# Row sums copied into the output page by ScalarE, and a new order of the first four slots, in a block attention with a gated MLP on one Trainium2 core

## Chip, cores and metric

The kernel runs on one core of one Trainium2 chip. The metric is the device time of one execution in microseconds (us). Three runs of the kernel before gave 791.10, 791.16 and 791.66 us; their median is 791.16 us. The profiled execution, from which all rows below come, took 792.08 us.

## What is computed

```
scores = q @ k.T / 8                     # 8 batches x 8 heads, 576 positions, head size 64
scores = where(block_i >= block_j, scores, -1e9)     # blocks of 64 positions
attn   = exp(scores - max) / (sum(exp) + 1e-9)
x      = attn @ v                        # heads side by side: 576 x 512 per batch

h      = gelu_tanh(x @ w_in)             # 512 -> 1024, halves u and v
v_n    = (v - mean) / sqrt(var + 1e-6) * g_ln
v_s    = w_sg @ v_n + b_sg               # over positions, 576 x 576
out    = x + (u * v_s) @ w_out
```

Inputs and outputs are 32-bit floats (two of the weights arrive as 64-bit and are narrowed in the kernel). Products need nearly full 32-bit precision, so most operands are split into a high and a low half of a rounded type, and a product is three matmuls: high by high, high by low, low by high.

## The kernel before, in words

**Slots.** Two heads of one batch make a pair; there are 32 pairs, and `slot(n, sc)` (line 743) works on pair n. A slot does two things at once: it finishes the attention of pair n (`Values`), and it makes the scores of pair n+1 (`Scores`). A batch is four slots. After the fourth slot of a batch, `begin` puts the batch's feed-forward part into a queue of generators, `work`, and each later call of `hole()` (line 722) in a slot issues one step of it, about a dozen or more matmuls. The first four slots have no such work: `hole()` does nothing there.

**Scores.** The 576 query rows lie in five tiles, 0 to 4. `step1` (S1) makes the first 288 columns of tile 4 and all of tile 1, `step2` (S2) the rest of tile 4, `step3` (S3) tiles 3 and 0, `step4` (S4) tile 2, each for both heads. The three terms of a product are issued in the order high-high, high-low (`k_l`), low-high (`q_l`). The result stands in a PSUM bank of tag `s` (five banks). VectorE takes the row maximum and writes the scores to SBUF (`maximum`, line 338); ScalarE makes the exponents and their sums (`exponents`). `split_qk` (line 127) makes the halves of the next pair's q and k: VectorE casts `qk_h`, then GpSimd subtracts to get `qk_l`, first for k and then for q. There is one buffer of each.

**Values.** TensorE transposes the exponents block by block into PSUM banks of tag `p` (three banks): `turn0` (bank `pa`, one for each head), `turn2` with `turn2_rest` (`pb`, two), `turn1` with `turn1_rest` (`pc`, two), `turn_first` (`pd`). ScalarE or VectorE copies each bank to SBUF (`pt`), and `av0`, `av2`, `av1`, `av00` multiply with v and accumulate in the bank `ob` (of tag `s`) and, for the first 64 rows, in columns 256 to 320 of `pd`, the tile `t4`. The inverse row sums are made by `inverse` at the start of a slot (VectorE `ri`, GpSimd `rx`), and `turn_sums` (line 461) transposes them into columns 128 to 256 of `t4` and into a bank `pe`, the tile `rp`. `normalise` (line 492) then has ScalarE copy `ob` and `o0` into a page `x` in SBUF, has VectorE multiply it with the sums in `pe` and `t4`, and stores the page to DRAM (`spill`). `split` (line 502) makes its halves `xh` (VectorE, with a small piece for the last rows by GpSimd) and `xl` (GpSimd) for the feed-forward part. Pages `x` share three buffers with `xr`, the pages that are loaded back for the residual.

**Order.** TensorE's instructions are kept in the order of the program (`PIN = "P"`, line 58). For the other engines a planner orders the instructions when the kernel is built, by readiness in its own simulation and, among ready ones, by program order. The engines then run these lists strictly in order. An instruction that waits holds up all that stand behind it on its engine. Dependencies inside PSUM are kept by bank: a write to one part of a bank waits for a read of another part of it.

**Weights.** They are loaded and narrowed in pieces, and `weight_step` issues one: for `w_in` that is a DMA, two instructions on ScalarE, three on VectorE and one on GpSimd. They stand behind the newest maximum and exponent that had been issued at that point. `load_share(n, k)` is called in a slot at four places, k = 0 to 3, and divides the slot's count `WS[n]` (2, 2, 2, 1 in the first four slots, 10 in slot 4) among them. With a count of two that is one piece at k = 1, in the slot's middle behind S1 and S2, and one at k = 3, behind `normalise`; the one of slot 3 comes at k = 3.

Of the kernel before, what the change touches and what calls it, by code (L numbers as in the profile page):

```python
# [9 lines left out]
F32 = mybir.dt.float32  # L10
# [4 lines left out]
ALU = mybir.AluOpType  # L15
# [13 lines left out]
def kernel(  # L29
# [13 lines left out]
    B, H, D, S = qT.shape  # L43
    P = 128
    BLK = 64
# [23 lines left out]
    def page(dtype, n, name):  # L69
        tag, bufs = KINDS.get(name, KINDS["w"])  # L70
        return sp.tile([P, n], dtype, tag=tag, name=name, bufs=bufs)

    def bank(tag, name, bufs):
        return psum.tile([P, 512], F32, tag=tag, name=name, bufs=bufs)

    def sbank(name):
        return bank("s", name, 5)

    def pbank(name):
        return bank("p", name, 3)  # L80
# [3 lines left out]
    def pin(ins, e):  # L84
        return tc.keep_in_program_order(ins) if e in kept else ins
# [4 lines left out]
    def turn(out, in_, identity):  # L90
        return pin(nc.tensor.transpose(out, in_, identity), "P")  # L91
# [11 lines left out]
    V, A, G, SP = Pinned(nc.vector, "V"), Pinned(nc.scalar, "A"), Pinned(nc.gpsimd, "G"), Pinned(nc.sync, "S")  # L103

    def copy(e, dst, src):
        return {"v": V.tensor_copy, "a": A.copy, "g": G.tensor_copy}[e](dst, src)
# [8 lines left out]
    def load_qk(n):  # L115
        b, h = PAIRS[n]
        if n == 0:

            q_f, k_f = page(F32, S, "w"), page(F32, S, "w")
        else:  # L120
            t = sp.tile([P, 2, S], F32, tag="qk_f", name="qk_f", bufs=1)
            q_f, k_f = t[:, 0, :], t[:, 1, :]
        SP.dma_start(q_f, qT[b, h : h + 2].rearrange("a d s -> (a d) s"))
        SP.dma_start(k_f, kT[b, h : h + 2].rearrange("a d s -> (a d) s"))
        qk[n] = (q_f, k_f) if n == 0 else t

    def split_qk(n):
        t = qk[n]
        hi = sp.tile([P, 2, S], F32R, tag="qk_h", name="qk_h", bufs=1)
        lo = sp.tile([P, 2, S], F32R, tag="qk_l", name="qk_l", bufs=1)  # L130
        V.tensor_copy(hi, t)
        for i in (1, 0):
            G.tensor_tensor(lo[:, i, :], t[:, i, :], hi[:, i, :].bitcast(F32), op=ALU.subtract)
        q_h, k_h, q_l, k_l = hi[:, 0, :], hi[:, 1, :], lo[:, 0, :], lo[:, 1, :]
        qk[n] = [(q_h, k_h), (q_h, k_l), (q_l, k_h)]

    def load_v(n):
        b, h = PAIRS[n]
        v_f = v_bufs[n % 2]
        cols = slice(h * D, (h + 2) * D)  # L140
        SP.dma_start(
            v_f[:, : NT - 1, :],
            v[b, : (NT - 1) * P, cols].rearrange("(j p) d -> p j d", p=P),
        )
        SP.dma_start(v_f[:TAIL, NT - 1, :], v[b, S - TAIL :, cols])
        vals[n] = v_f
# [6 lines left out]
    t = sbank("warm")  # L153
# [15 lines left out]
    for s in (0, 1):  # L169
        t = cp.tile([P, NT, 2 * D], F32, name=f"v_f{s}")  # L170
# [5 lines left out]
    for s in range(4):  # L176
        row = []
        for i in range(NT):
            t = cp.tile([P, P * (i + 1) if i else BLK], F32, name=f"prob{s}_{i}")
# [106 lines left out]
    def weight_step():  # L286

        with ExitStack() as stack:
            for ins in newest.values():
                stack.enter_context(tc.issue_after(ins.ins))  # L290
            while weights and next(weights[0][1], None) is None:
                weights.popleft()
# [96 lines left out]
    class Values:  # L389
# [71 lines left out]
        def turn_sums(self):  # L461

            turn(self.t4[:, 128:256], self.rx[:, 0, :], ident)
            t = self.rp = pbank("pe")
            for i in range(1, NT):
                turn(t[:, (i - 1) * P : i * P], self.rx[:, i, :], ident)

        def av(self, dst, j, pts, c0, n, start, stop):
            for a in (0, 1):
                r = slice(a * D, (a + 1) * D)  # L470
                mm(dst[r, :], self.v[:, j, r], pts[a][:, c0 : c0 + n], start=start, stop=stop)
# [19 lines left out]

        def normalise(self):

            x = self.x = page(F32, S, "x")
            copy("a", x[:, BLK:], self.ob)
            copy("a", x[:, :BLK], self.o0)
            V.tensor_tensor(x[:, BLK:], self.rp, x[:, BLK:], op=ALU.mult)
            V.tensor_tensor(x[:, :BLK], self.t4[:, 128:192], x[:, :BLK], op=ALU.mult)
            spill[self.b, self.p] = dp.tile([P, S], F32, tag="spill", name="spill", bufs=12)
            SP.dma_start(spill[self.b, self.p], x)  # L500

# [14 lines left out]
    def run_side(k):  # L516

        while k > 0 and side and side[0][0] != "G":
            k -= 1
            side.popleft()[1]()  # L520

    def run_gelu():

        if side and side[0][0] == "G":
            side.popleft()[1]()
# [196 lines left out]
    def hole(k=1):  # L722

        while k > 0 and work:
            try:
                next(work[0])
                k -= 1
            except StopIteration:
                work.popleft()

    WS = [2, 2, 2, 1, 10, 3, 3, 3, 2]

    def load_share(n, k):

        if n < len(WS):
            for _ in range(WS[n] * (k + 1) // 4 - WS[n] * k // 4):
                weight_step()

    PLAN = ["1111111", "1111111", "1111111", "1111112"]
# [3 lines left out]
    def slot(n, sc):  # L743
        va = Values(n, sc)
        nx = Scores(n + 1) if n + 1 < N else None
        g = [int(x) for x in (FIRST if n // 4 == 1 else PLAN)[n % 4]]
        if n + 2 < N:
            load_qk(n + 2)
        if n + 1 < N:
            load_v(n + 1)  # L750
        va.inverse()
        va.turn0(0)
        va.turn0(1)
        hole(g[0])
        load_share(n, 0)
        run_side(2)

        va.turn2()
        va.turn2_rest()
        if nx:  # L760
            nx.step1()
            nx.step2()
        va.av0()
        if nx:
            nx.exponents(1, 4)
        va.turn1()
        hole(g[1])
        load_share(n, 1)
        run_side(2)
        hole(g[2])  # L770
        run_side(2)
        va.turn1_rest()
        va.turn_first()
        if nx:
            nx.step3()
            nx.step4()
        va.av2()
        va.turn_sums()
        if nx:
            nx.exponents(3, 0, 2)  # L780
        hole(g[3])
        load_share(n, 2)
        run_side(2)
        va.av1()
        va.av00()
        hole(g[4])
        va.normalise()

        wait = n // (H // 2) > 0 and n % (H // 2) < 2
        pending.append(va.split)  # L790
        if not wait:
            while pending:
                pending.popleft()()
        run_side(2)
        if n + 2 < N:
            split_qk(n + 2)
        load_share(n, 3)
        hole(g[5])
        run_gelu()
        run_side(3)  # L800
        hole(g[6])
        run_side(3)
        if n % (H // 2) == 1:
            while pending:
                pending.popleft()()
        return nx
# [19 lines left out]
    for n in range(N):  # L826
        sc = slot(n, sc)
        if n % (H // 2) == H // 2 - 1:

            def begin(b=PAIRS[n][0]):  # L830
                v_, u_, s_, o_ = feed_forward(b)

                work.extend([v_, u_, *last_o, s_])
                last_o[:] = [o_]

            begin()
# [45 lines left out]
```

## Time and profile before

| | |
|---|---|
| median of three runs | 791.16 us |
| profiled execution | 792.08 us, of which the span from first to last instruction is 790.2 us |
| mean granted TensorE clock | 0.978 |
| slot 0 (first transpose to first transpose) | 9.83 to 25.51 us |
| slot 1, slot 2, slot 3 | 25.51 to 41.68, to 55.93, to 70.25 us |
| slot 4, the first with feed-forward steps | 70.25 to 106.45 us |
| VectorE and ScalarE busy, whole span | 63% and 57% |

A slot's limits are read from a timeline. Each row has a start in us, a duration, engine, line and operation, then what is written from what, the shapes and a count; a note in brackets gives the idle time of the engine ahead of it and what ended that. Almost all instructions carry line 88, 91 or 101, those of the helpers that record them, so rows are told apart by their tiles. The row of a stretch (`A:B`) gives its length, the busy time of each engine with its count of instructions, then the granted TensorE clock (1.00 is full), the share of the DMA engines and GB/s.

### The profile page before, as it was taken

What the parts mean: (1) busy time and instruction counts of PE and PEld (TensorE: products, weight loads), DVE (VectorE), ACT (ScalarE), POOL (GpSimd) and SP (SyncE); (2) the same over time, 40 slices, a digit from 0 to 9 for tenths busy, and PEclk for the clock granted to TensorE, in tenths of its full rate; (3) what the DMA queues carried; (4) which work ended last, traced back from release to release, by engine and by line L of the source; (5) the groups of instructions that cost most, each with busy time, mean ns of one, the idle gap of its engine ahead of it and who ended that gap; (6) DMA issues with size and microseconds to landing.
All of it is one profiled execution on the core that took longest, in us unless ns stands there. A gap on an engine that the chain in (4) does not pass through costs nothing. (4 is left out here: it accounts for less than half of the span.)

```text
span 790.2 us, 15821 instructions
## 1 busy us (share of the span) xinstructions
PE 761.1 (96%) x5926; PEld 639.9 (81%) x5926; DVE 499.7 (63%) x1457; ACT 450.0 (57%) x1172; POOL 267.9 (34%) x331
## 2 busy tenths in 40 slices
PE   7777998999999999999999999999999999999998
PEld 5554786877888888887888888888888978888998
DVE  5897578885757466563866648565676647633532
ACT  4775689567844478435974368544793358721600
POOL 4354255552424113351133414231233510322121
PEclk9897799999999999999999999999999999999999
DMA  7143224212241024311042122410233101320042
GB/s 239 61 126 118 89 91 141 88 61 75 78 149 60 2 76 122 106 61 52 25 136 90 61 76 62 145 50 32 77 106 121 61 19 59 105 76 31 1 121 75
DMA packets 46911, 65.66 MB, mean 83 GB/s; under 512 B 4082, under 2 KB 22514, under 8 KB 46836
## 3 DMA queue, kind: packets, MB, share of 16 engines
q1 hardware_dynamic: 46836, 64.67, 25.6%
q8 instruction: 46, 0.75, 0.4%
q14 instruction: 29, 0.24, 0.1%
HBM read 45.78 MB, written 18.87 MB: 82 GB/s over the span
## 5 line engine op out<-in xcount | busy, mean ns | idle before, releaser
L101 ACT ACTIVATE prob<-prob,negm 128x448 f32<-128x448 f32 (+4 forms) x320 | 176.4, 554 | 40.6 <-DVE negm L101 37.1
L101 POOL TENSOR_TENSOR qk_l<-qk_f,qk_h 128x576 fp32r<-128x576 f32 x62 | 90.9, 1486 | 229.7 <-PE pe L91 92.2
L101 DVE CUSTOM_DVE_ANT_0 prob<-s,mask 128x288 f32<-128x288 f32 (+2 forms) x320 | 117.1, 421 | 56.3 <-PE s L88 56.1
L88 PE MATMUL ob<-pt,v_f 128*64 128x512 f32 (+4 forms) x640 | 107.1, 448 | 0.0
L88 PE MATMUL s<-qk_h 64*128 64x288 f32 (+1 forms) x372 | 88.4, 341 | 3.9 <-ACT u L101 3.7
L101 POOL TENSOR_TENSOR gl<-u,gh 128x288 fp32r<-128x288 f32 x64 | 51.9, 812 | 113.4 <-DVE gh L101 80.2
L88 PE MATMUL s<-qk_l,qk_h 64*128 64x288 f32 (+1 forms) x372 | 83.0, 303 | 0.0
L88 PE MATMUL accu<-xh,wi_h 128*128 128x288 f32 x256 | 78.1, 305 | 0.0
L88 PE MATMUL accs<-ws_h,vh 128*128 128x288 f32 x256 | 78.1, 305 | 0.0
L88 PE MATMUL s<-qk_h,qk_l 64*128 64x288 f32 (+1 forms) x372 | 78.0, 300 | 0.0
L88 PE MATMUL acco<-gh,wo_h 128*128 128x288 f32 x256 | 77.6, 303 | 0.0
L88 PE MATMUL accu<-xl,wi_h 128*128 128x288 f32 x256 | 75.7, 296 | 0.0
L88 PE MATMUL accu<-xh,wi_l 128*128 128x288 f32 x256 | 75.5, 295 | 0.0
L88 PE MATMUL accs<-ws_l,vh 128*128 128x288 f32 x256 | 75.5, 295 | 0.0
L88 PE MATMUL accs<-ws_h,vl 128*128 128x288 f32 x256 | 75.5, 295 | 0.0
L88 PE MATMUL acco<-gh,wo_l 128*128 128x288 f32 x256 | 75.4, 294 | 0.0
L88 PE MATMUL acco<-gl,wo_h 128*128 128x288 f32 x256 | 75.3, 294 | 0.0
L88 PEld LDWEIGHTS ob<-pt,v_f 128*64 128x64 f32 x640 | 37.8, 137 | 41.2 <-issue 32.2
L88 PE MATMUL accv<-wi_h,xh 128*128 128x512 f32 x160 | 66.0, 412 | 3.3 <-POOL xh L101 3.3
L88 PEld LDWEIGHTS s<-qk_h 64*128 64x128 f32 x372 | 63.7, 188 | 5.9 <-ACT u L101 4.9
L88 PEld LDWEIGHTS s<-qk_h,qk_l 64*128 64x128 f32 x372 | 63.8, 187 | 0.0
L88 PE MATMUL accv<-wi_l,xh 128*128 128x512 f32 x160 | 63.8, 399 | 0.0
(104 smaller groups left out, 1924.2 us busy)
## 6 DMA issues: line engine op xcount, KB each, us to landing
spill<-x SPq DMA_DIRECT2D x32, 288.0 KB, 3.7
xr<-spill SPq DMA_DIRECT2D x32, 288.0 KB, 3.2
out_T<-xr SPq DMA_DIRECT2D x32, 288.0 KB, 3.0
qk_f<-in_qT SPq DMA_DIRECT2D x31, 288.0 KB, 3.4
qk_f<-in_kT SPq DMA_DIRECT2D x31, 288.0 KB, 3.8
v_f<-in_v SPq DMA_DIRECT2D x32, 256.0 KB, 3.1
raw<-in_w_in SPq DMA_DIRECT2D x16, 256.0 KB, 4.7
raw<-in_w_out SPq DMA_DIRECT2D x8, 256.0 KB, 5.2
```

The costliest lines, as they stand in the source:

```text
L88: return pin(nc.tensor.matmul(*a, **k), "P")
L101: return lambda *a, **k: pin(f(*a, **k), self.letter)
```

## The change

Three edits. First, `turn_sums` takes the page `x` and has ScalarE copy the transposed sums into it, from `pe` and from `t4`, right behind the transposes; `normalise` has VectorE multiply `ob` and `o0`, in PSUM, with the page. Second, in slots 0 to 3 (`n < H // 2`) `turn2` and `turn2_rest` stand behind S1, S2 and `av0` and no longer ahead of them. Third, in slots 0 to 3 all of a slot's weight pieces are issued at k = 1.

```diff
         def turn_sums(self):
 
             turn(self.t4[:, 128:256], self.rx[:, 0, :], ident)
-            t = self.rp = pbank("pe")
+            t = pbank("pe")
             for i in range(1, NT):
                 turn(t[:, (i - 1) * P : i * P], self.rx[:, i, :], ident)
+
+            x = self.x = page(F32, S, "x")
+            copy("a", x[:, BLK:], t)
+            copy("a", x[:, :BLK], self.t4[:, 128:192])
...
         def normalise(self):
 
-            x = self.x = page(F32, S, "x")
-            copy("a", x[:, BLK:], self.ob)
-            copy("a", x[:, :BLK], self.o0)
-            V.tensor_tensor(x[:, BLK:], self.rp, x[:, BLK:], op=ALU.mult)
-            V.tensor_tensor(x[:, :BLK], self.t4[:, 128:192], x[:, :BLK], op=ALU.mult)
+            x = self.x
+            V.tensor_tensor(x[:, BLK:], self.ob, x[:, BLK:], op=ALU.mult)
+            V.tensor_tensor(x[:, :BLK], self.o0, x[:, :BLK], op=ALU.mult)
...
         if n < len(WS):
-            for _ in range(WS[n] * (k + 1) // 4 - WS[n] * k // 4):
+            share = WS[n] * (k + 1) // 4 - WS[n] * k // 4
+            if n < H // 2:
+
+                share = WS[n] if k == 1 else 0
+            for _ in range(share):
                 weight_step()
...
-        va.turn2()
-        va.turn2_rest()
+        early = n < H // 2
+        if not early:
+            va.turn2()
+            va.turn2_rest()
         if nx:
             nx.step1()
             nx.step2()
         va.av0()
+        if early:
+            va.turn2()
+            va.turn2_rest()
         if nx:
             nx.exponents(1, 4)
         va.turn1()
```

## Prediction

> **What bounds the kernel now.** I read the page's busy shares first, then its 40 slices, then a table by slot.
>
> ```profile
> PE 761.1 (96%) x5926; PEld 639.9 (81%) x5926; DVE 499.7 (63%) x1457; ACT 450.0 (57%) x1172; POOL 267.9 (34%) x331
> PE   7777998999999999999999999999999999999998
> PEclk9897799999999999999999999999999999999999
> ```
>
> TensorE (PE) is busy for 761.1 of 790.2 us. From the sixth slice on it is full, so the later slots are bound by its own work, and the 29 us that it idles lie almost wholly in the first 100 us, where the granted clock is down as well. The table by slot says how much each has.
>
> ```profile
> 9.83:25.51 15.68, 11.84 (x98) 8.21 (x96) 13.30 (x51) 12.22 (x40) 6.00 (x7) 0.89 0.44 148
> 25.51:41.68 16.17, 13.14 (x99) 8.60 (x95) 13.30 (x41) 10.86 (x37) 7.09 (x9) 0.79 0.23 74
> 41.68:55.93 14.25, 11.63 (x100) 7.91 (x96) 12.61 (x39) 9.75 (x32) 7.29 (x10) 0.88 0.45 139
> 55.93:70.25 14.32, 11.59 (x99) 8.16 (x95) 11.74 (x35) 9.23 (x31) 6.26 (x8) 0.88 0.34 102
> 70.25:106.45 36.20, 30.99 (x180) 23.39 (x176) 22.51 (x63) 21.98 (x58) 18.84 (x21) 0.81 0.39 123
> ```
>
> No engine fills slots 1 to 3: PE idles 2.6 to 3.0 us in each, and VectorE (DVE), with 11.7 to 13.3 us busy, comes closest to being full. So a chain of waits sets their length. PE's waits up to 105 us and the timeline of PE at the start of slot 2 show where.
>
> ```profile
> PE pa L91 <- ACT pt L101: 6.1, 4, 1.9
> PE pb L91 <- DVE x L101: 3.7, 3, 1.4
> ```
> ```profile
> 41.68 0.66 PE L91 MATMUL pa<-ident,prob 128*128 128x128 f32 x4
> 43.64 0.66 PE L91 MATMUL pa<-ident,prob 128*128 128x128 f32 x4 [1.30 <-ACT pt L101]
> 45.61 1.08 PE L91 MATMUL pb<-ident,prob 128*128 128x128 f32 x7 [1.31 <-DVE x L101]
> ...
> 49.06 1.56 PE L88 MATMUL ob<-pt,v_f 128*64 128x512 f32 x4
> ```
>
> There are three `p` banks, and `pd` and `pe` are held until `normalise` is through. The first `pa` takes the one that is left, the second must wait until ScalarE (ACT) has copied the first out, and `pb` until DVE has multiplied by `pe`. The page's clock row falls for the same reason; a table in steps of 2 us has the clock at half behind these gaps, here and again in slot 4:
>
> ```profile
> 48.00:50.00 2.00, 2.00 (x12) 1.07 (x10) 1.81 (x11) 0.93 (x4) 0.33 (x1) 0.50 1.00 295
> 84.00:86.00 2.00, 2.00 (x6) 0.32 (x5) 1.97 (x10) 1.89 (x7) 0.00 (x0) 0.50 0.00 0
> ```
>
> The reason why DVE is late with `x` is in the lists of DVE, ACT and GpSimd (POOL) at the same boundary.
>
> ```profile
> 40.57 0.75 DVE L101 CAST qk_h<-qk_f 128x1152 fp32r<-128x1152 f32 x1
> 41.56 1.58 DVE L101 SCALAR_TENSOR_TENSOR w<-raw,w 128x256 uint32<-128x256 uint32 x1
> 43.07 1.36 DVE L101 TENSOR_TENSOR ri<-sums,tiny 128x10 f32<-128x10 f32 x1
> 44.87 0.68 DVE L101 TENSOR_TENSOR x<-pe,x 128x512 f32<-128x512 f32 x1
> 41.56 0.55 ACT L101 ACTIVATE prob<-prob,negm 128x320 f32<-128x320 f32 x1
> 42.44 0.56 ACT L101 COPY x<-ob 128x512 f32<-128x512 f32 x1
> 41.45 2.95 POOL L101 TENSOR_TENSOR qk_l<-qk_f,qk_h 128x576 fp32r<-128x576 f32 x2 [1.57 <-PE pe L91]
> ```
>
> `av00` is done at 41.68. ACT copies `ob` only at 42.44, behind its exponents, and DVE gets to the product only at 44.87, behind a weight piece and `ri`, both stretched while POOL subtracts (41.45 to 44.40).
>
> **The change, part by part.** *Copies.* The two ACT copies and the two DVE products keep their shapes, their counts (32 each) and one operand in PSUM, so I take their prices as unchanged (0.56 us for the large copy, 0.68 us for the large product) and no engine's total moves. What moves is their place. Behind `av00` there is then one product, not exponents, two copies and a product. Bank `pe` comes free in the old slot, so the second `pa` has a bank at once: the ACT wait goes, and what is late next is the last exponent itself. That exponent now stands behind two copies, about 0.6 us; pending behind it are the next slot's `ri` and second `pa`. With the old end of 41.56 + 0.55 = 42.11 it comes at about 42.7, so the second `pa` starts some 0.7 us earlier than 43.64.
>
> A new wait is added: `av00` writes `t4` and must wait for ACT's read of the sums in that bank. Behind it stands all of the next slot. In a slot with feed-forward work the cover is long:
>
> ```profile
> 318.98 0.60 PE L91 MATMUL pe<-ident,rx 128*128 128x128 f32 x4
> ...
> 322.00 0.29 PE L88 MATMUL pd<-pt,v_f 128*64 128x64 f32 x4
> ```
>
> From 319.58 to 322.00 are 2.4 us for one running exponent and the two copies (0.55 + 0.56 + some 0.2, by the rows above). I charge nothing there, with 1.5 us gained to 2 us lost over the 28 slots as bounds. In slots 0 to 3 the cover is only `av1`, about 1 us, so some 0.2 to 0.4 us of wait shows on PE; it isn't a link of the chain below, which leaves PE a microsecond at that place, and I charge nothing for it. That such waits go by bank and not by column is seen in slot 0, where the sums' transpose waits for ACT to read other columns of `pd`:
>
> ```profile
> 23.70 0.30 PE L91 MATMUL pd<-ident,rx 128*128 128x128 f32 x1 [1.04 <-ACT pt L101]
> ```
>
> *Order and pieces.* With no `pb` ahead of it, S1 follows the second `pa` at once, and its third term needs `q_l`. So the new slot is a chain from one end of the S4 maxima (call it D, 40.57 in slot 1) to the next. The rows that carry it, at full clock:
>
> ```profile
> 15.87 0.42 PE L88 MATMUL s<-qk_h 64*128 64x288 f32 x1
> 17.46 1.08 PE L88 MATMUL ob<-pt,v_f 128*64 128x512 f32 x4
> ```
> ```profile
> 63.88 1.08 PE L88 MATMUL ob<-pt,v_f 128*64 128x512 f32 x4
> 64.89 1.08 PE L91 MATMUL pc<-ident,prob 128*128 128x128 f32 x7
> 65.82 0.44 PE L88 MATMUL s<-qk_h 64*128 64x448 f32 x1
> ```
> ```profile
> 66.94 0.62 DVE L101 CUSTOM_DVE_ANT_0 prob<-s,mask 128x448 f32<-128x448 f32 x1 [1.59 <-PE s L88]
> 69.15 0.75 DVE L101 CAST qk_h<-qk_f 128x1152 fp32r<-128x1152 f32 x1
> 52.05 0.43 DVE L101 SCALAR_TENSOR_TENSOR w<-w 128x256 uint32<-128x256 uint32 x1 [0.92 <-ACT w L101]
> ```
>
> From D to `q_l`: 44.40 - 40.57 = 3.83 us. S1 and S2 take 1.59 us, of which four products of the first two terms run ahead, so 1.3 remain. `av0` 1.01; `pc` with `pd` 0.93, and `pb` alike; 0.3 for the second `pc`, which now follows `pb` directly and waits for ACT to empty its bank; from S3's first product to its first maximum 1.12; the maxima of S3 and S4 2.21. The sum is 3.83 + 1.3 + 1.01 + 0.93 + 0.93 + 0.3 + 1.12 + 2.21 = 11.6 us.
>
> DVE must fit in. S1's maxima can start about 0.95 us after `q_l`, at D + 4.8; at 2.2 us like those of S3 and S4 they end at D + 7.0; two weight pieces (three instructions of at most 0.43 each, about 1.1 in all) bring 9.2, a copy of `pb` (at most the 0.68 of the product, whose shape it has) 9.9, where the chain wants S3's maxima at 9.4. And a piece's last step waits 0.92 us for ACT. So a slot with two pieces is 12.1 to 13.0 us; I take 12.5. Slot 3 has only the gains, one cast: 12.0.
>
> | | before | after | bounds of the gain |
> |---|---|---|---|
> | slot 0 | 15.68 | 15.2 | -0.5 to 1.5 |
> | slots 1, 2, 3 | 16.17 + 14.25 + 14.32 = 44.74 | 12.5 + 12.5 + 12.0 = 37.0 | 2.5 to 9.8 |
>
> Slot 0 starts out of the prologue, so its second `pa` waits for the same exponents as now; half of the 1.04 us at `pd` goes because the maxima start sooner, and I bound it by that wait's whole and a little on either side. The lower bound for slots 1 to 3 has the half clock in each (1.75 us, worked out below), the upper one the bare chain of 11.6 us three times.
>
> The weights moved out of the boundary cost there nothing any more, and their DVE step leaves POOL's time (1.58 falls to 0.43); their DMAs are fetched four ahead on SP, so a piece in the middle finds its data. The spill on SP moves up with the product, and the load of k that is queued behind it.
>
> *Slot 4.* Its first feed-forward step needs the split of slot 3's page.
>
> ```profile
> 75.46 0.68 DVE L101 TENSOR_TENSOR x<-pe,x 128x512 f32<-128x512 f32 x1
> 78.46 0.32 POOL L101 TENSOR_TENSOR xh<-x,xh 128x64 fp32r<-128x64 f32 x1
> 78.83 0.80 PE L88 MATMUL accv<-wi_h,xh 128*128 128x512 f32 x1 [3.26 <-POOL xh L101]
> ```
>
> The product comes 5.2 us after the slot's start at 70.25, and `xh` 8.2 us after. With `ob` taken by DVE directly the product can come at 0.3 to 2 us (one or two weight steps may slip in ahead), its cast within a microsecond, and `xh` on POOL when `qk_l` is done, 2.7 to 4.1 us after the start. The `accv` row then stands at 3.2 to 6 us instead of 8.6: a gain of 2.6 to 5.4, and I take 4.3. The half clock that follows (0.50 still in the row from 84 us) costs half of what PE does in it from 78.83 us on, up to 4 us; I count 1.0 of it as recovered, because short gaps remain in front of it.
>
> The sum is 0.5 + 7.7 + 4.3 + 1.0 = 13.5 us. PE is full from there to the end, so it carries through. From the profiled 792.08 that gives 778.6; the median of the runs lies 0.9 lower, so I forecast 777.7 us.
>
> **The rivals.** *The clock stays at half* behind the remaining gaps. About 1.5 us of idle is left at each boundary (exponent, then `q_l`), spread over 4 us, where now 2.6 us lie. For it: the half clock came behind single gaps of only 1.30 and 1.31 us. Against: the sum of idle in the window is smaller. At 0.50, as in the row from 48 us, half of the time so run is lost; slot 2's mean of 0.88 over 14.25 us stands for 3.4 us of it, and so for 1.7 us lost; I count 1.75. Three slots lose 5.2, the recovery in slot 4 goes: gain 7.3, time 783.9.
>
> The Trainium skill (TensorE: Matmul & The Clock Gate, "HAM oscillation — how this bites in real kernels") warns of idle gaps above about 3.4 us. By that rule no boundary of slots 1 to 3 would lose its clock, and this rival had no chance; the trace, which has 0.50 behind gaps of 1.3 us, disagrees, and so I keep it.
>
> *The lists are the bound.* DVE has 12.6 us of work in slot 2, some of it stretched by POOL. If the planner puts the product ahead of the `qk_h` cast, or `xh` and `xl` ahead of `q_l`, D to `q_l` grows by 0.9 to 1.7 us; slots at 13.9, slot 4 with half its gain: 3 + 2 = 5 us, time 786. For it: all those steps become ready within a microsecond. Against: in the rows above the cast starts 1.1 us ahead of the end of `av00`.
>
> *Slower: `av00` waits for ACT's copies in the 28 later slots.* The place is the bank of `t4`. It decides from the point where ACT ends the copies more than 2.4 us behind the sums, for instance when the planner sets them behind the string of exponents, or when the page `x`, taken earlier, still belongs to an `xr` on its way out. At 0.6 us a slot it is 16.8 us, against a gain of 13.5 at most likely: 794.5. Even then each slot must lose 0.48 us before it outweighs the start; the 2.4 us of cover speak against it.
>
> *The change moves nothing that counts*: copies set behind the exponents in the first slots too, S1 no earlier because of `q_l`; 790 to 792. The two kinds of wait quoted at the start would both have to return elsewhere.
>
> **How the numbers follow.** Forecast 0.60, half clock 0.16, lists as bound 0.10, slower 0.08, nothing 0.06. The first three are faster, 0.86 in all; of the last I put 0.05 at the same and 0.01 beyond it, which makes slower 0.09. About 0.2% (1.6 us) is what a measurement of this kernel can tell from no change. Range: the upper bounds of the gains, 1.5 + 9.8 + 5.4 + 4 of which not all come together, give some 20 us and 771; the lower end takes in half clock and lists, with their own spread, at 788.
>
> **What would show it.** Right: `pa <- ACT pt` and `pb <- DVE x` gone from PE's waits up to 105 us; a new wait of `s` for POOL `qk_l` of about a microsecond; slots 1 to 3 at 12 to 13 us; the `accv` wait for `xh` under 2 us; PE's idle in the later slots unchanged. Wrong: PE waiting in `pd` for ACT `x` in later slots, clock at 0.50 in slots 1 to 3, or S3's maxima waiting behind weights.

## The result and the profile after

The changed kernel takes 786.4 us (median of six runs, 784.52 to 788.21), beside 791.41 us for the kernel before on the same chip: a ratio of 0.9938, 95% interval 0.992 to 0.9956. It is faster, by 5.0 us; 13.5 us were forecast. The profiled execution took 784.52 us, with a span of 782.7 us and a mean granted clock of 0.993, the fastest of the six.

The page's first rows for the changed kernel:

```profile
PE 755.5 (97%) x5926; PEld 636.3 (81%) x5926; DVE 486.8 (62%) x1457; ACT 448.0 (57%) x1172; POOL 270.3 (35%) x331
PE   7787998999999999999999999999999999999998
PEclk9999999999999999999999999999999999999999
```

The dips in the clock row (8, 7 and 7 in the second, fourth and fifth slice before) are gone. The table by slot, from first transpose to first transpose, shows that one stretch has grown all the same:

```profile
10.48:30.91 20.43, 14.27 (x97) 9.87 (x96) 14.43 (x54) 14.44 (x47) 7.27 (x9) 0.83 0.32 106
30.91:43.41 12.50, 10.96 (x99) 7.21 (x95) 9.93 (x38) 9.86 (x32) 6.88 (x9) 1.00 0.32 96
43.41:55.90 12.49, 10.95 (x100) 7.21 (x96) 10.02 (x38) 9.90 (x32) 7.40 (x10) 1.00 0.59 179
55.90:67.81 11.91, 10.67 (x99) 7.03 (x96) 9.46 (x37) 8.64 (x28) 5.43 (x7) 1.00 0.32 101
67.81:99.80 31.99, 27.86 (x180) 21.73 (x176) 21.95 (x59) 21.63 (x57) 20.06 (x21) 0.95 0.43 134
```

Slots 1 to 3 take 36.90 us instead of 44.74, at full clock. Slot 4 takes 31.99 instead of 36.20. Slot 0 takes 20.43 instead of 15.68. From slot 5 to the end the span is 782.7 - 99.80 = 682.9 us, and it was 790.2 - 106.45 = 683.75. PE's waits up to 105 us:

```profile
PE accv L88 <- POOL xh L101: 3.7, 1, 3.7
PE pc L91 <- ACT pt L101: 3.6, 1, 3.6
...
PE s L88 <- POOL sums L101: 1.9, 3, 0.6
...
PE pd L88 <- ACT x L101: 0.6, 3, 0.2
```

The two waits quoted before the change (`pa` for ACT's `pt`, `pb` for DVE's `x`) are no longer there. The row of `s` is the new wait for `q_l`: it names `sums`, which GpSimd clears as soon as `q_l` is done, but these matmuls read `q_l`. A wait of 3.6 us is new, and it is in slot 0. PE's rows on either side of it, and ACT's list in front of the copy that ends it:

```profile
20.15 0.55 PE L91 MATMUL pc<-ident,prob 128*128 128x128 f32 x3
24.25 1.20 PE L91 MATMUL pc<-ident,prob 128*128 128x128 f32 x4 [3.56 <-ACT pt L101]
```
```profile
19.44 0.45 ACT L101 ACTIVATE prob<-prob,negm 128x192 f32<-128x192 f32 x1 [0.25 <-DVE negm L101]
...
22.07 0.73 ACT L101 ACTIVATE w<-raw 128x256 f32<-128x256 f32 x2
...
22.97 0.74 ACT L101 CAST wi_h<-w 128x256 fp32r<-128x256 f32 x2 [0.17 <-DVE w L101]
23.62 0.58 ACT L101 COPY pt<-pb 128x512 f32<-128x512 f32 x1
```

The second `pc` needs the bank that `pb` holds until ACT has copied it. `pb` is transposed by 20.15, but ACT's copy stands behind the exponents of tiles 1 and 4 and both weight pieces, and begins at 23.62. In the kernel before, where `pb` came ahead of S1, the same copy stood ahead of all those:

```profile
16.62 0.56 ACT L101 COPY pt<-pb 128x512 f32<-128x512 f32 x1
18.14 0.41 ACT L101 CAST wi_h<-w 128x256 fp32r<-128x256 f32 x1 [0.97 <-DVE w L101]
19.40 0.46 ACT L101 ACTIVATE prob<-prob,negm 128x192 f32<-128x192 f32 x1 [0.85 <-DVE negm L101]
```

Behind the gap the clock is down. The table in steps of 2 us for the changed kernel:

```profile
22.00:24.00 2.00, 0.00 (x0) 0.00 (x0) 1.38 (x4) 1.83 (x7) 0.55 (x1) 1.00 0.01 4
24.00:26.00 2.00, 1.75 (x12) 1.42 (x14) 0.00 (x0) 0.54 (x2) 0.86 (x2) 0.55 0.04 8
26.00:28.00 2.00, 2.00 (x19) 1.77 (x19) 0.80 (x5) 1.01 (x4) 0.00 (x0) 0.60 0.00 0
```

Slot 0 has lost 4.75 us. PE idles 6.16 us in it (20.43 - 14.27) instead of 3.84 (15.68 - 11.84): 3.56 of new wait, while two old ones, of 1.04 us in `pd` and 0.19 us in `s`, are gone. And PE is busy for 14.27 us instead of 11.84, at a clock of 0.83 instead of 0.89. Not all of these 2.43 us need be clock: in e6 below, with the same order and a clock of 0.90, PE is still busy for 13.21 us in slot 0.

### The profile page after: what moved, and what is told of

Same layout as the page of the kernel before. It is cut to its first block, busy times and chain, and to the rows that moved or that the text cites. A ratio compares the mean times of both kernels' runs of the same rounds, so it can differ in the third digit from the quotient of the medians.

```text
span 782.7 us, 15820 instructions
## 1 busy us (share of the span) xinstructions
PE 755.5 (97%) x5926; PEld 636.3 (81%) x5926; DVE 486.8 (62%) x1457; ACT 448.0 (57%) x1172; POOL 270.3 (35%) x331
## 5 line engine op out<-in xcount | busy, mean ns | idle before, releaser
L88 PE MATMUL ob<-pt,v_f 128*64 128x512 f32 (+4 forms) x640 | 104.4, 437 | 0.6 <-ACT pt L101 0.5
L88 PE MATMUL s<-qk_h 64*128 64x288 f32 (+1 forms) x372 | 84.2, 338 | 3.7 <-ACT u L101 3.7
L88 PE MATMUL s<-qk_l,qk_h 64*128 64x288 f32 (+1 forms) x372 | 78.4, 299 | 0.0
L88 PE MATMUL s<-qk_h,qk_l 64*128 64x288 f32 (+1 forms) x372 | 73.5, 297 | 1.9 <-POOL sums L101 1.9
L101 ACT COPY pt<-pa 128x512 f32<-128x512 f32 x32 | 18.6, 580 | 84.1 <-PE pa L91 84.0
L101 DVE TENSOR_TENSOR xr<-acco,xr 128x288 f32<-128x288 f32 x64 | 29.2, 457 | 58.9 <-PE acco L88 48.7
L88 PEld LDWEIGHTS s<-qk_h 64*128 64x128 f32 x372 | 60.0, 184 | 6.3 <-ACT u L101 5.1
```

The lines of the kernel that those rows point to most:

```text
L88: return pin(nc.tensor.matmul(*a, **k), "P")
L101: return lambda *a, **k: pin(f(*a, **k), self.letter)
```

## Experiments

Times are medians of each kernel; ratios are to the kernel before, run on the same chip in between. Slots are from the profiled execution of each. The kernel before has medians from 791.41 to 792.0 us beside the several runs, so a difference of half a microsecond between two rows says little.

| kernel | copies | order | pieces | us | ratio, 95% interval | slot 0 | slots 1-3 | slot 4 |
|---|---|---|---|---|---|---|---|---|
| before | | | | 791.41 | 1 | 15.68 | 44.74 | 36.20 |
| e12_order | | x | | 791.97 | 0.9997, 0.9988 to 1.0006 | 19.98 | 41.67 | 34.45 |
| e10_weights | | | x | 783.23 | 0.9898, 0.9885 to 0.9911 | 16.00 | 38.48 | 31.94 |
| e1_copies | x | | | 782.07 | 0.9875, 0.9859 to 0.989 | 17.29 | 38.27 | 31.85 |
| e5_no_copies | | x | x | 787.68 | 0.9953, 0.9941 to 0.9966 | 21.75 | 36.60 | 33.48 |
| e2_no_weights | x | x | | 787.52 | 0.9943, 0.9929 to 0.9957 | 21.54 | 39.95 | 31.72 |
| e8_copies_weights | x | | x | 780.75 | 0.9855, 0.984 to 0.987 | 17.05 | 35.84 | 33.68 |
| the change | x | x | x | 786.4 | 0.9938, 0.992 to 0.9956 | 20.43 | 36.90 | 31.99 |

Theory: the shortfall is the second edit's doing, in slot 0, by way of the place of `pb`'s copy in ACT's list. Rivals: the copies cost something in their new place; the two pieces in the middle of slot 0 do; VectorE is late there whatever comes first.

**e1_copies.** The first edit alone; against the changed kernel:

```diff
-            if n < H // 2:
-
-                share = WS[n] if k == 1 else 0
...
-        early = n < H // 2
+        early = False
```

> The first edit alone: sums copied at turn_sums, order and weight pieces of the first slots as before. Theory (the early slots were bound by the chain through the p banks, and slot 0 of the changed kernel lost 5 us to its new order): slot 0 stays at 15.7 us and has no wait of the second pc; the wait of the second pa for ScalarE is gone in slots 1 to 3, but pb still comes ahead of S1, so these slots come to 13 to 13.5 us each, 4 us gained in all, and 787 us. Rival (the copies do harm of their own, in the later slots by the wait of av00, and the order makes the gain): 791 to 793 us, with waits of pd for ScalarE behind 100 us.

Measured: 782.07 us, 9.9 us under the kernel before on that chip (792.0) and 4.3 us less than all three edits together. The copies shorten slots 1 to 3 to 38.27 us without help, more than the 4 us expected. Slot 0 is 17.29 us and not 15.7, by the clock: it is 0.70 there in this profile, while PE idles only 2.79 us. The price of the new wait in `av00` shows here, since the old order leaves it less cover:

```profile
39.58 0.34 PE L88 MATMUL pd<-pt,v_f 128*64 128x64 f32 x4 [1.08 <-ACT x L101]
```

**e2_no_weights.** The changed kernel with the old shares:

```diff
-            if n < H // 2:
-
-                share = WS[n] if k == 1 else 0
```

> The changed kernel with the weight pieces shared out as before; copies and order as changed. Theory (slot 0's wait of 3.56 us of the second pc is due to pb's copy standing in ScalarE's list behind four exponents and two pieces): one piece fewer ahead of it takes 0.7 to 0.8 us off that wait, and slot 0 falls to about 19.5 us; slots 1 and 2 have a piece at their boundary again, stretched by GpSimd's subtraction, and grow from 12.5 to about 13.2; in all within 1.5 us of the changed kernel, 786 to 788. Rival (the pieces in the middle are the whole cause of slot 0's loss): slot 0 back at 15.7, 782 us.

Measured: 787.52 us. Slot 0 is 21.54 us with one piece in its middle instead of two, where 19.5 was expected: the wait of the second `pc` falls only from 3.56 to 3.22 us, and the clock of the slot is 0.76 in this profile. So the pieces are not what lengthened it. Slots 1 to 3 give back 3 us.

**e3_slot0_old.** The changed kernel, with order and shares of slot 0 as before:

```diff
-            if n < H // 2:
+            if 0 < n < H // 2:
...
-        early = n < H // 2
+        early = 0 < n < H // 2
```

> The changed kernel, but slot 0 keeps its old order of transposes and its old shares of weight pieces. Theory (slot 0's new order is where the forecast failed): slot 0 back to 15 to 15.7 us, slots 1 to 3 at 12.5, 12.5 and 11.9 as in the changed kernel, 781.5 us. Rival (slot 0's extra time only moves the prologue's delay and comes back in slot 1): slot 1 grows by some 4 us, 785 to 786 us.

Measured: 783.79 us, ratio 0.9897 (0.9883 to 0.991). Slot 0 falls to 16.96 us; slot 1 rises to 14.86 from 12.50, slots 2 and 3 hold. So the rival was right in part: 2.4 of the 3.5 us that slot 0 gains come back in slot 1.

**e6_pb_first.** The changed kernel, with one thing moved: in slot 0 ScalarE's exponents stand behind its copy of `pb` (`copied` is the last copy that `out` gave to ScalarE).

```diff
         if nx:
-            nx.exponents(1, 4)
+            with ExitStack() as stack:
+                if n == 0:
+                    stack.enter_context(tc.issue_after(va.copied.ins))
+                nx.exponents(1, 4)
```

> The changed kernel, with one thing moved in slot 0 alone: ScalarE's exponents of tiles 1 and 4 (and the weight pieces behind them) are issued behind its copy of pb. Theory A (slot 0 grew because that copy stands at the end of a list of four exponents and two pieces, and the second pc waits for it): the wait of 3.56 us goes, slot 0 falls from 20.4 to 16.5 to 17.5 us, slots 1 to 3 stay at 36.9, and the time is 782 to 784 us. Theory B (VectorE is late in slot 0 behind the prologue's two pieces, and the copy only shows it): another wait of about the same length takes its place (s or pd), slot 0 stays over 19 us, time 785 to 787 us.

Measured: 782.59 us, ratio 0.989 (0.9877 to 0.9904). ACT's copy and the table by slot:

```profile
20.17 0.59 ACT L101 COPY pt<-pb 128x512 f32<-128x512 f32 x1 [0.93 <-PE pb L91]
20.65 0.46 ACT L101 ACTIVATE prob<-prob,negm 128x192 f32<-128x192 f32 x1
```
```profile
10.52:27.61 17.09, 13.21 (x98) 8.74 (x96) 14.52 (x54) 13.16 (x45) 5.65 (x7) 0.90 0.38 129
```

The copy now waits for nothing but PE. The 3.56 us and the second stretch of low clock are gone. Slot 0 is 3.3 us shorter and the median 3.8 us lower. In the profiled execution, the slowest of the four, much of the gain is lost again: 0.7 us in slots 1 to 3, and 2 us behind slot 4, where the clock from 97 to 200 us is 0.97 instead of 1.00. This shows what the new wait is due to: the order is unchanged, and S1's first maximum is as late as in the changed kernel (18.71 and 18.67 us); the place in the list is another. VectorE's copy of the other `pb` came forward with it, from 23.19 to 21.57 us, so the run does not part the two copies. Slot 0 is still 1.4 us longer than in the kernel before.

**e8_copies_weights.** The changed kernel with the old order:

```diff
-        early = n < H // 2
+        early = False
```

> The copies, and the pieces of slots 0 to 3 in the middle, but turn2 in its old place ahead of S1. It separates the second edit from the third. If the order is what costs slot 0 its time: slot 0 near the 17.3 us of the copies alone, slots 1 to 3 at 37 to 39 us, 781 to 783 us. If the two pieces in the middle of slot 0 cost it: slot 0 at 19 us or more and 784 to 786 us.

Measured: 780.75 us. Slots 1 to 3 take 35.84 us, 1.06 less than with the new order. PE's rows at the start of slot 2 say why, first in the changed kernel, then in this one:

```profile
43.41 1.13 PE L91 MATMUL pa<-ident,prob 128*128 128x128 f32 x8
...
45.62 0.40 PE L88 MATMUL s<-qk_h,qk_l 64*128 64x288 f32 x2 [0.61 <-POOL sums L101]
...
47.69 1.27 PE L91 MATMUL pb<-ident,prob 128*128 128x128 f32 x10
48.88 0.55 PE L91 MATMUL pc<-ident,prob 128*128 128x128 f32 x3
```
```profile
39.23 0.95 PE L91 MATMUL pa<-ident,prob 128*128 128x128 f32 x6
...
40.82 1.02 PE L91 MATMUL pb<-ident,prob 128*128 128x128 f32 x7
...
41.94 0.29 PE L88 MATMUL s<-qk_h,qk_l 64*128 64x288 f32 x1
...
44.15 1.08 PE L91 MATMUL pc<-ident,prob 128*128 128x128 f32 x7
```

With the old order `pb` lies in the time in which PE waits for GpSimd's `q_l`, and costs nothing. With the new one PE stands 0.61 us for `q_l` and does `pb` afterwards: from slot start to `pc` it is 5.47 us against 4.92, and the second `pc` then waits another 0.70 us. Part of that is lost again in this kernel, to waits of 0.76 and 0.84 us for ACT later in the slot.

**e5_no_copies, e10_weights, e12_order.** Against the kernel before: the second and third edit as in the change's diff, the third alone, and the second alone.

> The changed kernel without its first edit: order and weight pieces as changed, normalise as before (ScalarE copies ob, VectorE multiplies by pe). Theory A (the copies carry the gain, and order with pieces costs some 3 us in slot 0): slot 0 again 20 to 21 us, slots 1 to 3 a little under the 44.7 us of before because pb no longer stands ahead of S1 (40 to 43 us), slot 4 as before at 36; 791 to 794 us. Theory B (copies and order are worth the same in any company): copies alone gave 9.3 us and all three edits 5.0, so order and pieces alone cost 4.3 us: 795 to 796 us. Theory C (order is what carries the gain of slots 1 to 3): those three sum to 37 to 38 us, and the time is 787 us or less.

> The third edit alone: only the pieces of slots 0 to 3 go to the middle; normalise and the order are as before. If the boundary of slots 1 to 3 is held by the place of VectorE's product behind a weight piece (one 1.58 us step and ri), the wait of pb for x falls from 1.3 us by about a microsecond in slots 1 and 2, and those slots lose 1 to 3 us in all with the clock: 788 to 790 us. If it is the chain through ScalarE's copy of ob, whatever stands on VectorE, nothing moves: 791 to 792 us. Either way it is a test of whether copies (9.3 us alone) and pieces add: with both 780.75 us came out, so 1.3 us for the pieces on top of the copies.

> The second edit alone: turn2 behind S1, S2 and av0 in slots 0 to 3, copies and pieces as before. It completes the table of the edits. Theory (the order only moves pb out of the shadow of the wait for q_l, and in slot 0 puts the copy of pb behind ScalarE's exponents): slot 0 at 19 to 21 us, slots 1 to 3 at 40 to 44 us, 790 to 795 us. Rival (the order by itself takes pb out of the queue for VectorE's product, and that is what shortened slots 1 to 3): those three at 36 to 38 us as with order and pieces together, 786 to 788 us.

Measured: 787.68, 783.23 and 791.97 us. In e5 theory C came nearest (36.60 us in slots 1 to 3), but order is not what carries it: without the pieces these slots take 41.67 us, without the order 38.48. Order alone moves nothing: what it gains in slots 1 to 4 (3.1 + 1.8 us) it pays in slot 0 (4.3). The pieces alone bring 8.6 us where I expected 1 to 3, without touching `normalise`. VectorE at the start of slot 2 there:

```profile
40.74 0.27 DVE L101 TENSOR_TENSOR ri<-sums,tiny 128x10 f32<-128x10 f32 x1 [1.30 <-ACT prob L101]
...
41.21 0.69 DVE L101 TENSOR_TENSOR x<-pe,x 128x512 f32<-128x512 f32 x1
```
```profile
26.52:38.97 12.45, 10.12 (x100) 6.86 (x96) 10.33 (x39) 9.69 (x32) 6.77 (x8) 1.00 0.31 97
38.97:51.41 12.44, 10.11 (x99) 6.86 (x96) 10.32 (x39) 9.69 (x32) 7.30 (x9) 1.00 0.57 180
```

The product comes 2.24 us after the slot's start (41.21 - 38.97) instead of 3.19 (44.87 - 41.68), the wait of `pb` for it is gone, and the clock of slots 1 and 2 is 1.00 instead of 0.79 and 0.88. Earlier copies keep the clock at 1.00 as well (e1), and the second cure on top of the first finds little left (e8 is 1.3 us below e1, and the times of each spread over about 3 us). The order by itself cures nothing of the product's lateness, 3.25 us after the start of slot 2 in e12, but takes `pb` out from behind it. Where the kernel before has two gaps of PE at the start of the slot, 1.30 and 1.31 us, one is left, and the clock stays at 1.00:

```profile
46.23 0.66 PE L91 MATMUL pa<-ident,prob 128*128 128x128 f32 x4 [1.36 <-ACT pt L101]
```
```profile
44.22:58.41 14.19, 11.54 (x98) 7.22 (x96) 12.53 (x39) 9.89 (x33) 7.28 (x10) 1.00 0.43 139
```

**e4_slot4, e7_copies_slot4, e9_best.** In slot 4 two of ten pieces leave the boundary. The line is added to the changed kernel, to e1 and to e8:

```diff
+            if n == H // 2:
+                share = [0, 5, 2, 3][k]
```

> The changed kernel, with the two pieces that slot 4 issues at its start put into its middle; one piece, which the first feed-forward step asks for, stays at the boundary. Theory (the split of slot 3's page stands behind weight pieces in the lists of VectorE and GpSimd): the wait of accv for xh falls from 3.7 us to 2 to 2.5, slot 4 from 32.0 to about 30.7, 785 us. Rival (GpSimd's subtraction for q and k alone sets the time of xh): the wait stays at 3.5 or more, no difference.

> The copies alone (old order, old places of the pieces in slots 0 to 3), and slot 4's ten pieces divided 0, 5, 2, 3 over its four places, so that two leave its boundary. The copies alone gave 782.1 us; the same division took 3.2 us off the changed kernel (786.4 to 783.2). If the two add, 779 us (778 to 780.5), with slot 4 at 30 to 30.5 us. If slot 4's gain hangs on the three slots ahead of it being short, 781 to 782 us.

> The copies, the pieces of slots 0 to 3 in the middle, the old order (which together gave 780.75 us), and slot 4's pieces divided 0, 5, 2, 3, so that the wait of the first accv for xh (3.5 us there) loses about 2 to 2.5 us as it did in the two kernels that had this division. Theory: 777 to 778 us, slots 1 to 3 at 35.8 us, slot 4 at 29.5 to 30.2 us. Rival: the pieces that stood in slot 4's middle and boundary only move and the time stays at 780 to 781 us.

Measured: 783.19 us (0.9891, 0.9878 to 0.9905), 779.89 us (0.9855, 0.9841 to 0.9868) and 777.91 us (0.9829, 0.9816 to 0.9841). The last one beats both kernels: copies, pieces in the middle, old order. Its slot 4:

```profile
63.56:92.93 29.37, 26.71 (x179) 20.60 (x176) 22.64 (x61) 21.33 (x58) 18.23 (x20) 1.00 0.50 145
```

**e11_changed_again.** The changed kernel, unaltered.

> The changed kernel itself, unaltered, on the chip of these runs, for a second count of its scatter: its six runs went from 784.52 to 788.21 us while the clock went from 0.993 to 0.980. If the scatter is the kernel's own (a clock that falls to half behind its gap in slot 0 at one time and not at another), a spread of 2.5 to 4 us again about 786 us, lower clock with longer time; if it was that chip's, a spread under 1.5 us.

Measured: 786.4 us again, 784.5 to 787.26. Its profiled execution took 787.26 us, with these rows in slot 0, PE's first and then those in steps of 2 us:

```profile
23.39 1.20 PE L91 MATMUL pc<-ident,prob 128*128 128x128 f32 x4 [2.68 <-ACT pt L101]
```
```profile
22.00:24.00 2.00, 0.61 (x3) 0.50 (x3) 1.02 (x3) 1.22 (x3) 1.40 (x2) 0.57 0.01 4
24.00:26.00 2.00, 2.00 (x19) 1.75 (x18) 0.00 (x0) 1.21 (x3) 0.00 (x1) 0.50 0.04 8
26.00:28.00 2.00, 2.00 (x16) 1.37 (x15) 1.66 (x9) 1.01 (x5) 0.00 (x0) 0.50 0.00 0
28.00:30.00 2.00, 2.00 (x15) 0.99 (x13) 1.29 (x5) 2.00 (x10) 0.57 (x1) 0.72 0.00 0
```

The same gap, 2.68 us long here, has more low clock around it than in the first profile, and slot 4 took 34.57 us at 0.85. So the scatter came again on other runs. Between the two profiles 2.6 us of it lie in slot 4 and 1.0 in slot 0. Other kernels point to slot 4 as well: e4 has slot 0's gap of 3.56 us and 1.7 us in slot 4, and its four runs lie within 0.25 us (783.17 to 783.42); e8 has no such gap in slot 0 and 3.5 us in slot 4, and its four spread from 778.34 to 781.48. e9, which has neither gap at that length, stays within 777.3 to 778.44. These are four to six runs of each, and e6's profile shows a low clock elsewhere too, so this is not settled.

## Why the prediction was right in sign and too large

- **The step that failed: slot 0, forecast 0.5 us of gain, bounds -0.5 to 1.5; measured 4.75 us of loss.** The prediction asked there only what the second `pa` and `pd` wait for. The wait of the second `pc` for the copy of `pb` stood in its chain for slots 1 to 3 at 0.3 us, and in slot 0 it was put at nothing. There it is 3.56 us: `pb`'s copy moved with `pb` and now stands behind the exponents and two pieces on ACT. "The maxima start sooner" was right but small: in slot 0 VectorE is busy with the prologue's two pieces, and S1's first maximum starts 8.19 us after the slot's start (18.67 - 10.48) instead of 8.80 (18.63 - 9.83). That is 0.6 us, where the copy comes 7.0 us later (23.62 instead of 16.62). The lists were read at slot 2's boundary alone; those of slot 0, with the prologue's pieces in them, were not laid out. e6 shows the cause: with the copies of `pb` ahead of the exponents the wait is gone, and 3.3 us of slot 0 with it.
- **Slots 1 to 3: forecast 37.0 us, measured 36.90, and in part by luck.** The bare chain came to 11.6 us, and 0.9 was added because VectorE had to fit two pieces in ahead of S3's maxima. It does fit them in, and waits for PE there. What is longer is PE's way from `pb` to S3: 3.36 us (47.69 to 51.05), where the chain had 0.93 + 0.93 + 0.3 = 2.16. The second `pc` waits for VectorE's copy of `pb`, not for ACT's:

```profile
50.13 0.94 PE L91 MATMUL pc<-ident,prob 128*128 128x128 f32 x7 [0.70 <-DVE pt L101]
```
```profile
52.20 0.62 DVE L101 CUSTOM_DVE_ANT_0 prob<-s,mask 128x448 f32<-128x448 f32 x1 [1.12 <-PE s L88]
```

  What was not asked is what the slot would be with the old order. It is 35.84 us for the three (e8): `pb`, entered in the chain at 0.93 us, lay in the wait for `q_l` before. Of the 7.84 us gained about half is PE's idle time (8.38 to 4.32 us); the rest is its busy time (36.36 to 32.58) at a clock of 1.00 instead of 0.85. Busy time does not go by the clock alone: at 1.00 too it is 30.57 us in e8 and 34.77 in e12 for these slots.
- **Slot 4: forecast 4.3 us by the wait and 1.0 by the clock; measured 4.21, with the shares the other way round.** PE's idle falls by 1.08 us (5.21 to 4.13), its busy time by 3.13, at 0.95 instead of 0.81. The `accv` wait was to be under 2 us and is 3.73. The row that it holds up comes 6.8 us after the slot's start (74.64 - 67.81); it was to come after 3.2 to 6, and came after 8.6 before. The lists of DVE and GpSimd show why:

```profile
66.98 0.69 DVE L101 TENSOR_SCALAR w<-raw 128x256 uint32<-128x256 uint32 x3
67.59 1.08 DVE L101 SCALAR_TENSOR_TENSOR w<-raw,w 128x256 uint32<-128x256 uint32 x3
...
70.39 0.62 DVE L101 TENSOR_TENSOR x<-ob,x 128x512 f32<-128x512 f32 x1
...
72.75 0.98 DVE L101 CAST xh<-x 128x576 fp32r<-128x576 f32 x1
```
```profile
72.44 1.88 POOL L101 TENSOR_TENSOR wi_l<-w,wi_h 128x256 fp32r<-128x256 f32 x2
74.28 0.31 POOL L101 TENSOR_TENSOR xh<-x,xh 128x64 fp32r<-128x64 f32 x1
```

  I had allowed for one or two weight steps ahead of the product; there are three pieces at this boundary, and their GpSimd halves stand ahead of `xh` as well. With two of them moved (e4) the wait is 1.7 us, the clock of the slot 1.00, the slot 30.17 us, and the kernel 3.2 us faster.
- **The later slots: no gain and no loss charged.** 682.9 us against 683.75. The other kernels with the copies take 683.0 to 683.1 there (e6 684.85), those without 683.8 to 684.4, so the copies may gain a little. PE idles 0.8 us more there (10.74 us against 9.90) and is busy for less. The rival that would have made it slower, `av00` behind ACT's copies, did not come there. In the first slots the wait was put at 0.2 to 0.4 us; it is 0.2 with the new order and up to 1.08 with the old one (e1).
- **The clock.** The rival of a half clock in slots 1 to 3 did not come. It came in slot 0, behind the new gap. That gap is 3.56 us in one profile and 2.68 in the other, and behind both the rows show a clock of 0.50 to 0.60 before it comes back. The Trainium skill (TensorE: Matmul & The Clock Gate, "HAM oscillation — how this bites in real kernels") warns of gaps above about 3.4 us. The first gap agrees with that; the second is shorter, and the clock fell as well.
- **From profile to median.** The forecast put the median 0.9 us under the profiled run, as before. The median of the changed kernel is 1.9 us above its profiled run, so 2.8 us of the shortfall lie between profile and median. The profiled run was the fastest of the six; the others have lower mean clocks, 0.980 to 0.989 beside 0.993, and the sum held the clock of this step constant.

The shortfall against 777.7 us is 8.7 us, but for rounding: 5.25 in slot 0, 1.1 in slot 4, 0.65 in a later first transpose (10.48 against 9.83; over all profiles it lies between 9.41 and 10.69), 2.8 from profile to median, less 0.1 in slots 1 to 3 and 0.9 in the later ones.

What stays open is why slot 0 is some 1.4 us longer than before in the other kernels with copies, too. In e8 (17.05 us) `av00` waits 0.84 us there for ACT's copies, and `pd` 1.36 instead of 1.04; neither was tried by itself. In e1 (17.29) `av00` waits only 0.18 us, and it is the low clock that lengthens the slot. In e6 (17.09) PE idles as long as before, 3.88 us, and is busy for longer.

## What to carry to other kernels

When a step is moved behind another, lay out the list of the engine that frees its buffer, in the first iteration as well as in the steady one: the copy moves with the step, and here it went behind four exponents and two weight pieces. Before you put a step behind a wait, ask whether it was not what filled the wait. And try edits that share a cause one by one: pieces alone gave 8.6 us, copies alone 9.9, both 10.8, and the new order took more than 5 us of it away.

## What the runs showed of the hardware

One TensorE gap of the same program costs differently from run to run: the kernel's times spread over 3.7 us (784.52 to 788.21) with the mean granted clock between 0.980 and 0.993, and the two profiles show clocks of 0.83 and 0.68 in slot 0, 0.95 and 0.85 in slot 4, for the same instructions. Without gaps of that length the spread is 1.1 us (e9). Two gaps of 1.30 and 1.31 us close together were followed by a clock of 0.50 (slot 2 before), two of 0.81 and 1.16 us (e10) or one of 1.36 us (e12) by 1.00.

A small VectorE addition (`ri`, 128x10) took 1.36 us in the kernel before (43.07 to 44.43) and 0.27 us in e10 (40.74 to 41.01), both while GpSimd was subtracting `qk_l` in two instructions. GpSimd's second in the kernel before, and its first in e10:

```profile
42.83 1.58 POOL L101 TENSOR_TENSOR qk_l<-qk_f,qk_h 128x576 fp32r<-128x576 f32 x1
```
```profile
39.58 1.40 POOL L101 TENSOR_TENSOR qk_l<-qk_f,qk_h 128x576 fp32r<-128x576 f32 x1 [0.75 <-PE pd L88]
```

They end at 44.41 and 40.98 us, and `ri` ends 0.02 and 0.03 us later. So do all `ri` of 0.27 us or more in the first 100 us of the kernel before, the changed kernel and e10: each ends 0.02 to 0.04 us behind the end of a subtraction. The length is what was left of the subtraction when `ri` came, which bears out the prediction's reading that `ri` is stretched while GpSimd subtracts. It is not always `ri` that waits: one of 0.16 us at 98.27 in the kernel before lies inside a subtraction that takes 2.11 us itself.
